# A new order of the same tasks for a fused attention and FFN kernel, from a replay with other transpose times

## The chip, the cores and the metric

The kernel runs on one core of a Trainium2 chip. The time is the device time of one execution in microseconds. TensorE (PE) multiplies matrices, VectorE (DVE), ScalarE (ACT) and GpSimd (POOL) do the rest, and SyncE (SP) issues the transfers.

## The reference

One pre-norm transformer layer on 2048 tokens of width 640, in bf16: multi-query attention with 32 query heads of 20 elements that share one key and one value head, then a gated FFN of width 1536.

```python
q = (x @ wq).reshape(B, S, H, Dh)...          # H = 32, Dh = 20
k = x @ wk;  v = x @ wv                       # one head for all
p = softmax(einsum("bhqd,bkd->bhqk", q, k) * Dh ** -0.5)
attn = einsum("bhqk,bkd->bhqd", p, v)... @ wo
ffn  = (gelu(x @ w_gate) * (x @ w_up)) @ w_down

h  = x + attn(layernorm(x))
h2 = h + ffn(layernorm(h))
```

## The kernel before

The 2048 tokens are cut into 16 tiles of 128 (t = 0 to 15). A *pass* (t, h) is one tile of queries with half of the heads. Its scores are computed transposed, in units of 128 keys by 4 heads of 128 queries (512 columns, one PSUM bank). A *cycle* n is a group of up to five units: `qk_n_0` and `qk_n_1` are its score matmuls on TensorE (line 1257), and `exp_n_0` and `exp_n_1` the exponentials on ScalarE (line 1365) that read two or three banks at once. There are 313 cycles. A part of the keys of each pass (five blocks of 128 in most) takes another way. Its scores (`qkd_n`) become 16-bit patterns of the exponential on VectorE (`db_n`, line 1313), of which two more copies with shifted exponents are made (`ds1_n`, `ds2_n`), either on VectorE (line 1324) or on GpSimd (line 1330). Matmuls with three weighted copies of v (`v_w0` to `v_w2`, GpSimd, line 1933) then sum the three terms.

`pv` are the products with v (line 1481), which gather in one PSUM bank for each pass. At its end `t1`, `rl` (VectorE) and `on` (GpSimd) normalise it, and a DMA transpose turns both halves of a tile (`oT_t`). The output projection `wo` follows on TensorE, then the second layer norm, its transpose `bT_t`, the gate and up matmuls `g` and `u`, the gelu (`sq`, `zk`, `z`, `th`, `h1`, `ph`), a transpose of the product `hT_t`, the down projection `dn` and the store `out_t`.

At the start each tile of x is loaded, normalised (statistics `as1`, `as2` and `aag`, reciprocal `arc`, result `anm_t`), turned by a DMA transpose (`aT_t`) or, for tiles 0, 1 and 5, by TensorE (`atp`, evicted by `ate`), and projected to k and v (`kv_t`, evicted by `ke_t` and `vee_t`). Queries are projected per tile and turned by `qT_t`. All transposes and loads of this kind go through SP's queue, one behind the other. Where TensorE would stand idle there are matmuls on constants, called `warm` and `filler`.

The order of the work on each engine is fixed when the program is built. A planner (`schedule`) first makes an order. `reorder` then replaces it by an order written out in strings: `MOVES` for each engine, `LEFT` for the ds that change between VectorE and GpSimd and for fillers that are dropped, `HEADS` for the head that each `qkd` takes. `retime` replays that order with durations and gives every task a start time; from these come the choice between the two auxiliary PSUM banks (5 and 7), the semaphore waits, and the places at which the streams of SP, ScalarE and GpSimd are split into two blocks. In this replay a transfer that starts before 70 us takes the planner's own duration. A later one took

```python
REAL_DMA = {"qT": 4.6, "bT": 4.0, "oT": 4.1, "hT": 5.0, "out": 4.5}
...
dur = t.dur if at < 70 else self.REAL_DMA.get(t.name.split("_")[0], t.dur)
t.end = landed[e] = max(at + dur, landed[e] + t.serve)
```

where `t.serve` is the least time between two landings of one queue, 0.65 us for the layer norm's transposes. The engines run their streams in order, and each instruction waits on semaphores for what it reads.

Of the kernel before, what the change touches and what calls it, by code (L numbers as in the profile page):

```python
# [15 lines left out]
        "000000000000010000002100101001000161014423010022010432310230553103617279001081106553161006404005"  # L16
        "0444033100"
    ),
    "act": (
        "000000000000001001000200000000000000000000000000000000000000000000000000000000000000000000000000"  # L20
        "00000000000000000000000Y000000000000000000000000000000000J00000000000000000000000000000000000000"
        "000000000000000000g000000000000000000000000000000000000000000000000000d0000000000000000000000000"
        "0000000000000000000000n000000000000000000000000000000000000000000D000000000000000000000000000000"
        "00000Z1300000000000000000000000000000Z1400000000000000000000000000000000000000000000000000000000"
        "00000Z1100000000000000000Z10000000000000000000000000000000000000000000000Z1c000000000000000V0000"
        "0000000000000000000000000000000000Z1300000000000000000000J00000000000000000000000000000000000091"
        "10112000"
    ),
    "pe": (
        "000000000000000000000000000000020011000112543000101152007113210101093210120021333321213399921154"  # L30
        "921242262b123333325e21a3k20111c30300p055Z1hgg5876l665aZ136d77kZ138l8et877686i66e56k6065w70583030"
        "03i006312l0232i222222200b1ag5bmf5na00300008a000a7ooooof11dd1dd223k732b200a2ni322524e32n62120008S"
        "WWZ12Z12m212001k080Z1aZ1aZ1a0Z1bZ1b3i00eu2y024840252Z1UZ1UZ1V3dZ1TZ1V001021r7100q9024061b0Z1IZ1I"
        "Z1K31181wZ1EZ1E43110f00199a608800k08edc0gec103000uaaaccpppp0V09TTUU20m8h1f925nnppp2g011d1511vvvA"
        "2zKK6JLL20711UVVVV260b62c0014Z24Z24Z26Z29Z291Z2qZ2s14Z2qZ2qZ2q10730Z2o0Z2nZ2nZ2nZ2n4d07h02600o10"
        "02c5f40d40Z20Z20g31130Z1UZ1V5o0Z1S030838631051d01b007e1c003000b0301he03488823080eeeff040lllln363"
        "c54Z2lZ2lZ2lZ2nZ2nZ2nZ2nZ2oZ2oZ2oZ2qZ2q5c412b25201c0200Z2gZ2iZ2iZ2i0a0Z2fZ2fZ2fZ2hZ2hZ2hZ2mZ2m26"
        "33f102775061182Z29Z29Z29Z29Z292401Z2bZ2bZ2d1Z2cZ2d12060Z2oZ2oZ2oZ2o10Z2m37708Z2hZ2hZ2hZ2h21bZ2eZ"
        "2eZ2e54060011174384c02321101f1c2e01j22222222Z1BZ1BZ1C02331Z1x223200Z1r0Z1qZ1q42Z1oZ1oZ1oZ1tZ1t22"
        "013e434318j16i8066966600000833g30C02AC23AA4091Z103Z0ZZ11Z11Z12148043a1731yy20254v1uv4242QUUYZ102"  # L40
        "310306802Z1WZ1X0Z1WZ1W01Z2234308400Z2hZ2hZ2hZ2hZ2h7465741Z20Z20Z20Z20Z20c272812j0000a9034Z1OZ1PZ"
        "1P52Z1NZ1N101804036620677771a0020Z1qZ1qZ1qZ1qZ1q070bbbbb07260091b041g2Z19Z192Z18k52Z15Z157k1e9w8"
        "888880c9h578c95777956fma7i5f7555i5de7000003912j00600b3360a390g6a0101lu41t1879912505142332330d01c"
        "0g111057424171617121nn1400jjjl05jjkkk1j6g01a33334400cjfs1F00DD4444500wbv602b08jjjjj0kkq14o221n10"
        "LMM25KK332aZ11Z11Z114eZ11Z157554551438402118a010Z1cZ1d0Z1dZ1dZ1e7301r210x1s1E33331hZ1XZ1X037Z1U3"
        "Z1TZ1TZ1VZ1V14Z1TZ1TZ1UZ1UZ1U042960QQQk630MM5329140h45978995d71430241130b55044407fZ1b01Z19Z190Z1"
        "8Z18Z1aZ1a04Z1a6Z19Z19Z19Z1906631003410lmmmm611UU1c25QQQ1110000681Z14Z14Z14Z14Z163211182142Z10Z1"
        "0Z102b4Z0ZZ0Zf31Z1sZ1s44Z1qZ1tZ1t0231320090Z1B40Z1BZ1BZ1B00Z1z66004307Z2tZ2tZ2tZ2v040Z2sa8203422"
        "41250129614222III6c20JJ33i0026431191060n0e400001ffi3104db65000005003240jjjjj31101tttttZ2HZ2HZ2HZ"
        "2HZ2HZ2H28Z2F51Z2DZ2JZ2M6Z2LZ2NZ30Z30Z32Z32Z32574Z2ZZ2ZZ2ZZ2ZZ30Z303Z2Z452810Z1FZ1HZ1HZ1IZ1I3271"  # L50
        "126840704Z4aZ4aZ4a61Z48Z49164202500Z405Z3ZZ3Z73Z3YZ3Y0732756435Z2xZ2xZ2zZ2zZ2z68Z3HZ3HZ3HZ3HZ3H1"
        "92438221355535105821Z3rZ3rl52Z3oZ3oZ3o700a0092ag16dh06cf55b000800b75500000011Z1G1Z1FZ1GZ1G114Z1I"
        "Z1LZ1LZ1N1Z1MZ1MZ1MZ1M20330405770672303iiiiiZ1OZ1OZ1PZ1PZ1PZ1PZ1PZ1PZ1PZ1PZ1PZ1P523631f225601c5Z"
        "2KZ2KZ2KZ2KZ2K73640145Z2JZ2JZ2JZ2JZ2J06522133000222Z2oZ2oZ2pZ2qZ2q630125990714Z2jZ2j2bZ2hZ2hZ2h3"
        "703121070Z2jZ2kbj1a38Z2eZ2gZ2g0240624001aZ3KZ3KZ3KZ3KZ3KZ3QZ3Q1sZ3OZ3OZ3OZ3TZ3T43717366621521h31"
        "5666c60208Z3BZ3CZ3CZ3CZ3CZ3EZ3E03Z3CZ3CZ3EZ3EZ3E0563035052Z1HZ1HZ1K071Z1H0Z1J30e0Z3jZ3jZ3j010Z3g"
        "Z3g2e00200000hhllp053Z2ZZ2ZZ2ZZ2ZZ2Zb465142Z5dZ5eZ5eZ5eZ5gZ5gZ5g341Z5dZ5fZ5fZ5fZ5g441d6022834302"
        "241128Z4XZ4XZ4XZ4XZ4ZZ4Z1210Z4W4Z4VZ4VZ4WZ4W202a5Z4R10203204192522204180d06Z1Y0Z1X06Z20Z20Z20220"
        "131h171m01h6d0h20Z1S1060dZ1NZ1N5Z1MZ1M6d5aK6hw6g6f6ptk65000006Akssd7gpppahlcb0aaeaZ1mZ1maZ1rZ1uZ"
        "1vb555550648m60000434a93b24e0f3932225Z17Z172Z18Z18Z1921Z2m107Z2lZ2lZ2lZ2l78d030Z2qZ2qZ2qZ3xZ2qZ2"  # L60
        "q40Z3te0Z3rZ3w5Z3v44000223101a1330Z3oZ3oZ3oZ3o2Z3q345Z1RZ1RZ1RZ1RZ1R25556432404dddee0651553Z3iZ3"
        "iZ3l131Z3iZ3k3Z3QZ3QZ3QZ3QZ3Q0Z3P0Z3OZ3OZ3OZ3OZ3OZ3O22Z3GZ3MZ3MZ3OZ3OZ13Z13Z13Z13Z133650Z3IZ3I2Z"
        "3HZ3HZ3JZ3J15Z3HZ3HZ3IZ3IZ3LZ3L7421532431BBBBF283338334202554052Z3hZ3hZ3iZ3iZ3i2441Z3zZ3zZ3zZ3zZ"
        "3z45Z3AZ3CiZ3BZ3D1154Z3zZ3zZ3z110411130e23200209Z3nZ3nZ3n9Z3mZ3m010Z3jZ3jZ3jZ3jZ3jZ3j30Z3h45780h"
# [2079 lines left out]
```

## Time and profile before

| | before |
|---|---|
| median of 3 runs | 732.18 us (729.44 to 733.83) |
| the profiled execution's own time | 730.82 us |
| its span, first to last instruction | 727.4 us |
| busy: TensorE, ScalarE, VectorE, GpSimd | 98%, 95%, 93%, 63% of the span |
| mean granted TensorE clock | 0.998 |
| ScalarE's waits for score matmuls, whole span | 11.5 us in 21 waits |
| transposes on SP's queue | 75 |

All rows come from one profiled execution, and times in them count from its first instruction. In a row of the timeline stand start, length, engine, line, operation, what is written from what, the shape and the number of instructions merged, and in square brackets the idle time before with the one that ended it. A short stall of ScalarE in the middle of the kernel costs its own length, unless a later wait would have held ScalarE anyway.

### The profile page before, as it was taken

How to read it: one execution, taken by the hardware profiler on the slowest of the kernel's cores; microseconds unless marked ns; L12 is line 12 of the kernel's file. 1: busy time of each engine (PE TensorE's matmuls, PEld its weight loads, DVE VectorE, ACT ScalarE, POOL GpSimd, SP SyncE). 2: the span in 40 equal slices, each digit the busy share in tenths (PEclk: the TensorE clock that was granted, in tenths of full speed). 3: DMA queues.
4: the chain of work that ended last, by engine and by line, in shares of the span. 5: the costliest groups of instructions: out<-in, count | busy, mean ns of one | idle time of the engine just before them, and what ended most of it. 6: DMA issues, size and time to landing. Idle time of an engine off the chain costs nothing.

```text
span 727.4 us, 24310 instructions
## 1 busy us (share of the span) xinstructions
PE 709.4 (98%) x10816; PEld 271.5 (37%) x10816; DVE 676.3 (93%) x1261; ACT 691.8 (95%) x667; POOL 459.5 (63%) x366
## 2 busy tenths in 40 slices
PE   8889999999999999999999999999999999999998
PEld 3433333333333333333343434433343333333336
DVE  7878989999999999999999999999999999999895
ACT  4999999999999999999999999999999999999982
POOL 4347483876476867968857565787468765872131
PEclk9999999999999999999999999999999999999999
DMA  6858201112110103030101221121240121012202
GB/s 171 138 184 238 25 2 21 23 27 42 34 25 2 28 6 66 3 58 3 30 23 23 44 23 31 23 49 11 33 57 11 21 53 41 20 11 34 51 5 42
DMA packets 79949, 31.50 MB, mean 43 GB/s; under 512 B 70880, under 2 KB 78560, under 8 KB 79840
## 3 DMA queue, kind: packets, MB, share of 16 engines
q1 hardware_dynamic: 78528, 29.86, 20.6%
q8 instruction: 85, 1.39, 0.9%
q10 hardware_dynamic: 1312, 0.05, 0.1%
q14 instruction: 24, 0.20, 0.1%
HBM read 10.21 MB, written 2.62 MB: 18 GB/s over the span
## 4 chain that ended last, share of the span: by engine, by line
PE 67%; ACT 22%; DVE 5%; DMA 4%; POOL 2%; issue 0%; SPq 0%; DVEq 0%; POOLq 0%
PE ps L900 23%; ACT pbuf L1365 21%; PE ps L1257 21%; PE ps L1481 21%; DVE dbuf L1313 2%; DMA xnT<-xn_tmp 2%; POOL dbuf L1330 1%; DMA onT<-oN 1%; DMA xh<-in_A_x_dram 1%; PE ps L1823 1%; ACT g_z L1646 1%; DVE dbuf L1324 1%; PE ps L1078 0%; PE ps L1842 0%; DVE stats L997 0%
## 5 line engine op out<-in xcount | busy, mean ns | idle before, releaser
L1365 ACT ACTIVATE pbuf<-ps 128x1536 bf16<-128x1536 f32 (+1 forms) x626 | 663.8, 1182 | 12.9 <-PE ps L1257 11.5
L1330 POOL TENSOR_TENSOR dbuf<-dbuf,shifts 128x1024 int32<-128x1024 int32 x170 | 319.7, 1894 | 149.0 <-PE ps L1481 66.9
L1313 DVE TENSOR_SCALAR dbuf<-ps 128x512 int16<-128x512 f32 x608 | 391.5, 683 | 20.8 <-PE ps L1257 17.4
L1257 PE MATMUL ps<-qT,kT 32*128 32x512 bf16 x2048 | 273.2, 385 | 7.7 <-ACT pbuf L1365 2.6
L1481 PE MATMUL ps<-dbuf,v_w 128*32 128x512 bf16 x1824 | 165.0, 384 | 1.0 <-POOL v_w L1933 0.9
L1257 PEld LDWEIGHTS ps<-qT,kT 32*128 32x128 bf16 x2048 | 72.2, 91 | 222.2 <-ACT pbuf L1365 98.1
L1481 PE MATMUL ps<-pbuf,v_ext 128*32 128x512 bf16 (+3 forms) x1928 | 131.0, 329 | 0.4 <-ACT pbuf L1365 0.2
L1324 DVE TENSOR_SCALAR dbuf<-dbuf 128x2048 int16<-128x2048 int16 x134 | 89.9, 698 | 0.6
L1481 PEld LDWEIGHTS ps<-dbuf,v_w 128*32 128x32 bf16 x1824 | 44.1, 95 | 62.3 <-issue 41.4
L900 PE MATMUL ps<-wd_sb,hhT 128*32 128x320 bf16 x1440 | 65.8, 301 | 1.5 <-DVE g_z L1866 0.8
L900 PE MATMUL ps<-wu_sb,xnT 128*32 128x512 bf16 x900 | 64.8, 382 | 0.0
L900 PE MATMUL ps<-wg_sb,xnT 128*32 128x512 bf16 x900 | 63.4, 382 | 0.2
L1481 PEld LDWEIGHTS ps<-pbuf,v_ext 128*32 128x32 bf16 x1928 | 41.5, 95 | 56.6 <-issue 37.7
L1634 POOL TENSOR_TENSOR g_z<-g_gs 128x512 bf16<-128x512 bf16 x45 | 46.5, 1039 | 14.2 <-DVE g_gs L1632 14.0
L1606 POOL TENSOR_TENSOR g_us<-g_z,g_us 128x512 bf16<-128x512 bf16 x24 | 27.4, 1155 | 26.9 <-DVE g_z L1649 26.9
L900 PEld LDWEIGHTS ps<-wd_sb,hhT 128*32 128x32 bf16 x1440 | 33.3, 96 | 24.1 <-issue 9.3
L1640 DVE SCALAR_TENSOR_TENSOR g_us<-ps,g_gs 128x512 bf16<-128x512 f32 x45 | 30.8, 684 | 1.6 <-PE ps L900 1.0
L900 PE MATMUL ps<-wq_sb,xnT 128*32 128x320 bf16 (+1 forms) x660 | 31.3, 297 | 0.3 <-DMA wq_sb<-in_A_wq_dram 0.3
L1632 DVE CAST g_gs<-ps 128x512 bf16<-128x512 f32 x45 | 30.6, 682 | 1.0 <-PE ps L900 0.7
L1507 POOL TENSOR_TENSOR oN<-oT,rL 128x320 bf16<-128x320 f32 x30 | 21.8, 727 | 15.0 <-DVE rL L1502 14.9
L900 PEld LDWEIGHTS ps<-wg_sb,xnT 128*32 128x32 bf16 x900 | 19.2, 95 | 24.5 <-issue 6.8
L1003 POOL TENSOR_SCALAR lnve<-mv 128x1 bf16<-128x1 f32 x31 | 6.8, 222 | 33.6 <-DVE mv L1001 33.3
(117 smaller groups left out, 407.5 us busy)
## 6 DMA issues: line engine op xcount, KB each, us to landing
out_dram<-xh SPq DMA_DIRECT2D x15, 160.0 KB, 2.0
wg_sb<-in_B_w_gate_dram SPq DMA_DIRECT2D x1, 1920.0 KB, 7.4
wd_sb<-in_B_w_down_dram SPq DMA_DIRECT2D x1, 1920.0 KB, 15.6
wu_sb<-in_B_w_up_dram SPq DMA_DIRECT2D x1, 1920.0 KB, 20.0
xh<-in_A_x_dram SPq DMA_DIRECT2D x2, 640.0 KB, 7.3
xh<-in_A_x_dram SPq DMA_DIRECT2D x3, 320.0 KB, 3.2
wq_sb<-in_A_wq_dram SPq DMA_DIRECT2D x2, 400.0 KB, 4.9
wo_sb<-in_A_wo_dram SPq DMA_DIRECT2D x1, 800.0 KB, 9.3
```

Source lines behind the costliest of these rows:

```text
L900: ins = e.matmul(out[r, :], lhs[:, r], rhs, start=start, stop=stop, tile_position=(0, 32 * b))
L1257: return e.matmul(bk.rearrange("p (g n) -> p g n", g=4), kT4[r, kt * P:(kt + 1) * P], qT[r, main_q[t].index, 4 * h:4 * h + 4, :], start=Tr ...
L1313: quad["bits"].append(sc.add("dve", lambda e: e.tensor_scalar(part(seg, w=slice(512 * item[0], 512 * item[0] + 512)), bk(), D_BIAS, 0.0, A ...
L1324: dep = [sc.add("dve", lambda e, j=j, s=s: e.tensor_scalar(part(s), part(seg), D_SHIFT[j], None, ALU.add), 0.602, bits + t_shift, prio=0.4 ...
L1330: dep[0].other = (lambda e, j=j, s=s: e.tensor_tensor(pairs(s), pairs(seg), shifts[:, j - 1:j].to_broadcast([P, 1024]), ALU.add), 2.03)
L1365: exps.append(sc.add("act", lambda e, w0=w0, w1=w1, to=to: e.activation(pbuf[:, to:to + w1 - w0], ps[:, w0:w1], ACT.Exp, scale=EXP_SCALE), ...
L1481: ins = e.matmul(ps[32 * b:32 * b + 32, PVB * 512 + a:PVB * 512 + a + n].rearrange("p (a n) -> p a n", n=32), x[2], span.rearrange("p (a n ...
L1507: onorm[(t, h)] = c = sc.add(by, lambda e: e.tensor_tensor(oN[:, otk.index, h * (D // 2):(h + 1) * (D // 2)].rearrange("p (g l d) -> p l g ...
L1606: return [sc.add("pool", lambda e, c=slice(512 * j, 512 * j + 512): e.tensor_tensor(out[:, k.index, c], a[:, k.index, c], b[:, k.index, c] ...
L1632: ge = sc.add("dve", lambda e, col=col, bk=bk: e.tensor_copy(g_gs[:, gsl.index, col], bk()), d_ps(512), [gm], prio=EVAC + pr, rel=[ax], na ...
L1634: sqt = sc.add("pool", lambda e, col=col: e.tensor_tensor(g_z[:, gsl.index, col], g_gs[:, gsl.index, col], g_gs[:, gsl.index, col], ALU.mult),
L1640: uts.append(sc.add("dve", lambda e, col=col, bk=bk: e.scalar_tensor_tensor(g_us[:, gsl.index, col], bk(), 0.5, g_gs[:, gsl.index, col], A ...
```

## The change

The new order strings are another permutation of the same tasks, with these differences in what runs: three fillers more are kept (127 instead of 130 dropped), 119 instead of 114 ds go from VectorE to GpSimd (17 the other way in both), and 294 of 484 `qkd` take their heads in another sequence. The search that found the order isn't in the file. It used the replay below, and charged early stretches with little TensorE work more. The replay gets new transfer times, one for a transfer alone and one for the distance to the landing before it on the same queue:

```diff
 MOVES = {
     "sp": (
-        "000000000000010000002100101001000161014423010022010432310230553103617279001081106553161006404005"
-        "0444033100"
+        "000000000000010000001000221022100100400330010023200031120031044200257016801007006504205006450005"
+        "0544033100"
     ),
...
-    REAL_DMA = {"qT": 4.6, "bT": 4.0, "oT": 4.1, "hT": 5.0, "out": 4.5}
+    REAL_DMA = {"qT": 3.2, "bT": 3.5, "oT": 2.9, "hT": 4.4, "out": 2.2}
+    BEHIND_DMA = {"qT": 2.3, "bT": 2.0, "oT": 1.6, "hT": 2.6, "out": 0.9}
...
-                dur = t.dur if at < 70 else self.REAL_DMA.get(t.name.split("_")[0], t.dur)
-                t.end = landed[e] = max(at + dur, landed[e] + t.serve)
+                kind = t.name.split("_")[0]
+                late = at >= 70 and kind in self.REAL_DMA
+                t.end = landed[e] = max(at + (self.REAL_DMA[kind] if late else t.dur),
+                                        landed[e] + (self.BEHIND_DMA[kind] if late else t.serve))
```

Decoded, the orders begin to differ as follows (old above new in each pair):

```
TensorE  qk_0_0 warm warm warm warm kv_1 warm warm qk_0_1 qk_1_0 kv_2 atp_5 kv_3 qk_1_1
         qk_0_0 warm kv_1 warm warm warm warm warm qk_0_1 qk_1_0 kv_2 atp_5 kv_3 atp_5 qk_1_1
VectorE  as1_5 aag_3 as2_5 arc_2 qe_0_0 aag_5 as1_4 ate_1 qr_0 ... vee_3 arc_6 ke_3 anm_6
(second) as1_4 aag_3 arc_2 qe_0_0 as1_5 as2_5 ate_1 qr_0 ... ke_3 arc_6 as1_9 arc_7 anm_6 vee_3
GpSimd   ds2_12 v_w0 v_w1 ds1_12 v_w2 ds1_14 ds2_14
         v_w0 v_w1 v_w2 ds1_12 ds2_12 ds2_14
ScalarE  exp_0_0 vee_1 ke_1 exp_0_1 vee_2 ke_2 exp_1_0 exp_1_1 ate_5
         exp_0_0 ke_1 vee_1 exp_0_1 ke_2 vee_2 exp_1_0 ate_5 exp_1_1
SP       qT_0 aT_15 aT_14 qT_1 wg wo wd wu qT_2 oT_0 qT_3 bT_0
         aT_15 aT_14 qT_0 qT_1 wu wd wg wo oT_0 bT_0 qT_3 qT_2
```

(qe_0_0 and qr_0 are the eviction and the turned copy of the first queries.) From there to the end tasks change places with near neighbours.

178 lines of the change are left out of this document (89 added, 89 removed).

## The prediction

> **What bounds the kernel now.** I read the summary of the page first, then the busy times by stretch, then the waits of ScalarE, then the chain of waits, and last the instructions in order of time around each place where the chain leaves ScalarE.
>
> ```profile
> span 727.4 us, 24310 instructions
> PE 709.4 (98%) x10816; PEld 271.5 (37%) x10816; DVE 676.3 (93%) x1261; ACT 691.8 (95%) x667; POOL 459.5 (63%) x366
> ...
> L1365 ACT ACTIVATE pbuf<-ps 128x1536 bf16<-128x1536 f32 (+1 forms) x626 | 663.8, 1182 | 12.9 <-PE ps L1257 11.5
> ```
>
> ScalarE (ACT) is busy 691.8 of 727.4 us, nearly all of it in 626 exponentials of 1.18 us. Its instructions are the same in number and shape after the change, so 691.8 us is a floor, and only the 35.6 us in which it stands idle can be won. The stretches show where they lie (columns: length, then PE, PEld, DVE, ACT and POOL busy, granted TensorE clock, DMA share, GB/s).
>
> ```profile
> 0.00:20.00 20.00, 16.38 (x216) 7.81 (x216) 15.19 (x55) 10.29 (x22) 9.41 (x33) 0.91 0.62 167
> ...
> 550.00:600.00 50.00, 49.50 (x783) 18.87 (x787) 48.44 (x87) 47.20 (x45) 37.88 (x29) 1.00 0.16 30
> ...
> 710.00:727.00 17.00, 13.78 (x239) 11.24 (x235) 9.56 (x27) 4.30 (x8) 1.53 (x2) 1.00 0.31 45
> ```
>
> The first 20 us hold 9.7 us of it, the last 17 us 12.7 us. Between 50 and 700 us ScalarE waits for TensorE only this much:
>
> ```profile
> ACT pbuf L1365 <- PE ps L1257: 7.6, 18, 1.0
> ```
>
> So there are three accounts: the start, 7.6 us in 18 small waits in the middle, and the end. An order can gain a few us in all; it can lose more, since TensorE is 98% busy and takes its work strictly in the written order.
>
> **The change part by part.** The sum is made against the profiled execution, 730.82 us, which is 3.42 us more than its span; the median of the runs, 732.18, is 1.36 us above it, and I add that at the end. What moves is read out of the order strings, each decoded against the planner's list of tasks.
>
> First, GpSimd near 45 us. Its old order is ds2_12, v_w0, v_w1, ds1_12, v_w2; the new one is v_w0, v_w1, v_w2, ds1_12, ds2_12.
>
> ```profile
> 43.20 1.89 POOL L1330 TENSOR_TENSOR dbuf<-dbuf,shifts 128x1024 int32<-128x1024 int32 x1 [10.93 <-DVE dbuf L1313]
> 45.06 1.33 POOL L1933 TENSOR_SCALAR v_w<-v_ext 128x160 bf16<-128x160 bf16 x2
> 46.36 1.89 POOL L1330 TENSOR_TENSOR dbuf<-dbuf,shifts 128x1024 int32<-128x1024 int32 x1
> 48.21 0.61 POOL L1933 TENSOR_SCALAR v_w<-v_ext 128x160 bf16<-128x160 bf16 x1
> ...
> 48.88 0.40 PE L1481 MATMUL ps<-dbuf,v_w 128*32 128x512 bf16 x4 [0.94 <-POOL v_w L1933]
> ...
> 49.86 74.89 ACT L1365 ACTIVATE pbuf<-ps 128x1024 bf16<-128x1024 f32 x71 [0.68 <-PE ps L1257]
> ```
>
> TensorE stands 0.94 us for v_w2, and the next exponential starts 0.68 us late. GpSimd was idle for 10.93 us before ds2_12, so three v_w of about 0.65 us fit into that gap once the evicted v that they read is there. The two ds of 1.89 us then end near 47.0 us (43.20 + 2 x 1.89), before the 48.88 at which the matmul on them ran. What is late next is the last matmul on ds2_12 near 47.1, ahead of the exponential's need. Gain 0.68 us; its bounds are 0 (another wait at that place) and 0.94. After this row ScalarE runs for 74.89 us without a gap, so the gain stays in ScalarE's line at least as far as 124.75 us.
>
> Second, the start. TensorE takes kv_1 after one warming group instead of four; five more follow it, where two did. DVE drops one of two statistics ahead of the cast that the first scores wait for. Neither can be booked as a gain, because ScalarE is held again at 24.37 us:
>
> ```profile
> 12.12 1.45 ACT L1365 ACTIVATE pbuf<-ps 128x1536 bf16<-128x1536 f32 x1 [2.25 <-PE ps L1257]
> 15.34 1.02 ACT L1365 ACTIVATE pbuf<-ps 128x1024 bf16<-128x1024 f32 x1 [1.16 <-PE ps L1257]
> 24.37 24.82 ACT L1365 ACTIVATE pbuf<-ps 128x1536 bf16<-128x1536 f32 x22 [0.52 <-PE ps L1257]
> ...
> 17.63 0.18 DVE L1095 CAST v_ext<-ps 128x20 bf16<-128x20 f32 x1 [0.90 <-PE ps L1080]
> 17.98 0.44 DVE L1018 TENSOR_SCALAR xn_tmp<-xh,mv,lnr 128x640 bf16<-128x640 bf16 x1
> 18.45 4.93 DMA xnT<-xn_tmp
> 23.43 0.45 PE L1078 MATMUL ps<-xnT,wk 128*128 128x128 bf16 x5 [0.78 <-DMA xnT<-xn_tmp]
> ```
>
> The chain there is kv_3, its eviction on DVE at 17.63, the normalisation anm_6 at 17.98, the transpose aT_6 that lands 4.93 us later, kv_6, then qk_4_0. In the new order DVE does ke_3, arc_6, as1_9 and arc_7 between kv_3 and anm_6, where it did vee_3, arc_6 and ke_3. That is one statistics instruction more, and I take 0.4 us for it, from the nearest row on DVE, anm_6 with 0.44. Against it stands an earlier kv_3: DVE idles 0.90 us for it, and the reshuffle before it brings between 0.1 and 0.9. The net is between 0.5 us gained and 0.4 lost. I take 0.15 us lost, near the slower end, because the next rows show most of the reshuffle to run at a reduced clock.
>
> ```profile
> 12.00:14.00 2.00, 2.00 (x33) 1.17 (x34) 2.00 (x7) 1.62 (x3) 0.81 (x3) 0.77 0.36 72
> 14.00:16.00 2.00, 2.00 (x17) 0.47 (x10) 2.00 (x10) 0.84 (x3) 0.47 (x3) 0.50 0.49 95
> 16.00:18.00 2.00, 1.74 (x29) 1.30 (x30) 1.10 (x6) 1.83 (x4) 1.05 (x2) 0.88 0.67 135
> ...
> 13.72 1.04 PE L900 MATMUL ps<-halves,zeros 128*32 128x512 bf16 x8
> ```
>
> The granted clock falls to 0.50 near 13 us and returns by 17. Two warming groups take 1.04 us in it. Five groups at half that each are 2.6 us, so if the clock falls at the same moment the new qk_0_1 starts no earlier than the old. The three fillers more than before (16 instead of 13) lie beside exponentials; at this halved pace they would cost 1.6 us of TensorE, which the 24.37 us hold covers, and if that cover went they would delay one exponential. [...]
>
> Third, the transposes. The replay's times are cut (turned attention output 4.1 to 2.9 us alone, and 1.6 behind another), and the order is moved to fit. What the trace shows from issue to landing (median over all; then the minimum, median and maximum of onT alone):
>
> ```profile
> xnT<-xn_tmp SPq DMA_TRANSPOSE x28, 2.9
> qT<-q_tok SPq DMA_TRANSPOSE x16, 3.2
> onT<-oN SPq DMA_TRANSPOSE x16, 2.6
> hhT<-g_us SPq DMA_TRANSPOSE x15, 3.9
> ...
> DMA to landing us min/median/max: 2.3/2.6/4.6
> ```
>
> The new figures lie just above the medians, the old ones near the maxima. On TensorE the first output projection of a tile comes half a cycle (one exponential, 1.18 us) earlier in tiles 1, 5, 6 and 7 and half a cycle later in tiles 4 and 12. The rest of the projections and FFN groups shift by about a quarter of a cycle on average. On SP's queue qT_0 goes behind aT_15 and aT_14, the weights go wu, wd, wg, wo instead of wg, wo, wd, wu, qT_2 goes behind oT_0, bT_0 and qT_3, and several qT and out transfers swap with their neighbours.
>
> ```profile
> 46.98 6.90 SPq L952 DMA_DIRECT2D wu_sb<-in_B_w_up_dram  x1
> 69.32 1.20 SPq L1514 DMA_TRANSPOSE onT<-oN  x1
> ...
> wu_sb<-in_B_w_up_dram SPq DMA_DIRECT2D x1, 1920.0 KB, 20.0
> ```
>
> The last of the four weight loads landed at 67.0 us (46.98 + 20.0), ahead of the first oT at 69.32 that the first weight, wo, has to meet. They move the same bytes, so wo as the last lands near 67 too. If that 2.3 us of cover went, the first projection would wait for wo. qT_0 is wanted only by the second pass and qT_2 only by tile 2, after all of tile 1. I book nothing for these.
>
> One case can be followed. The worst waits of the middle come from here (rows of the chain of waits, then of TensorE and ScalarE):
>
> ```profile
> 566.37 5.59 POOL dbuf L1330 x3
> ...
> 572.67 4.57 DMA onT<-oN
> ...
> 577.38 0.86 PE L900 MATMUL ps<-wo_sb,onT 128*32 128x320 bf16 x20 [0.34 <-DMA onT<-oN]
> ...
> 576.30 3.36 ACT L1365 ACTIVATE pbuf<-ps 128x1536 bf16<-128x1536 f32 x3 [1.01 <-PE ps L1257]
> 580.30 2.37 ACT L1365 ACTIVATE pbuf<-ps 128x1024 bf16<-128x1024 f32 x2 [0.64 <-PE ps L1257]
> ```
>
> Three ds on GpSimd stand ahead of on_12_1, then its transpose takes 4.57 us. The new order puts a fourth ds (1.86 us each, 5.59 / 3) ahead of on_12_1 and moves the projection back by 1.18. So the projection would wait 0.34 + 1.86 - 1.18 = 1.0 us if the transpose is as slow again, and not at all at the median of 2.6. Bounds for ScalarE are 1.0 lost and 1.65 gained (its two waits, 1.01 + 0.64); I take 0 for this place, between them. For the middle as a whole I take 0 too: the new 2.9 us still leave 0.3 to the median of 2.6, and the two ends are the outer rivals below.
>
> Fourth, five more ds go from DVE to GpSimd (net; some change places). GpSimd gains 5 x 1.86 = 9.3 us on 459.5 busy, DVE loses work. Neither bounds a stretch quoted above, so 0.
>
> Fifth, the end. The new order evicts u14_8 between the two hc_15 on DVE and moves wb1_15 ahead of the first gate matmuls.
>
> ```profile
> 716.44 1.81 PE L900 MATMUL ps<-wd_sb,hhT 128*32 128x320 bf16 x48 [0.78 <-DVE g_z L1866]
> 721.73 3.42 PE L1842 MATMUL ps<-wd_sb,hhT 128*128 128x320 bf16 x24
> ```
>
> TensorE's work in the tail is the same, and both places where it waits or closes (the down projection of tile 14 behind a bank that g_z frees, and the last 24 matmuls) keep their predecessors. I book 0, between 0.5 lost and 0.5 gained.
>
> Sum: 730.82 - 0.68 + 0.15 = 730.29 on the profiled execution; with 1.36 to the median, 731.65, told as 731.6 us. About 0.5% (3.66 us) is what a measurement of this kernel can tell from no change.
>
> **The rivals.**
>
> Faster: the truer transposes let the middle waits go. Two thirds of the 7.6 us vanish, 5.0 us, and the v_w gain stays: 731.6 - 5.0 = 726.6. For it: the waits are small, 18 in number, and the longest follow one late projection. Against it: TensorE itself is 98% busy, and in the stretch from 550 us, where the waits are densest, 49.50 of 50 us.
>
> Slower: the transposes are now given so little time that TensorE, which can't pass a waiting projection, stands before it. The place is the first output projection of tiles 1, 5, 6 and 7. Each is 1.18 us earlier, and a projection that already met its data at the landing hands all of that to ScalarE: 4 x 1.18 = 4.7 us, or 731.6 + 4.7 = 736.3. It decides once those onT take over 2.9 us to land instead of the median 2.6; the 4.57 above shows that some do.
>
> The clock: another early stretch falls under the reduced clock, or the same one lasts longer. In the three stretches above TensorE lost 2 x (0.23 + 0.50 + 0.12) = 1.7 us; a second such dip that nothing covers gives 733.3. [...]
>
> No effect: the edited times touch only the replay, and the orders, being permutations of the same tasks, leave all 18 waits as they are, v_w included: 732.2.
>
> **How the numbers follow.** My forecast gets 0.38, with 729.6 to 733.6 as its own range (the bounds of the start, the projection and the end, 2 us each way). No effect gets 0.08 and the clock 0.15; all three lie within 0.5%, together 0.61. Faster gets 0.20 and slower 0.19. The range reaches into both outer cases, to 727.2 and 736.0, about half of each.
>
> **What would show it.** Right: no wait for v_w near 48 us; the exponential at 24.37 us held by the landing of aT_6 as before, within 0.5 us; the middle waits between 5 and 10 us; the last exponential about 0.5 us earlier. Wrong: waits of TensorE on onT, xnT or hhT of over 1 us in several tiles (slower), or a middle account under 3 us (faster). A dip of the clock beyond 18 us would speak for the clock.

## The result: no change that can be told

| | before | after |
|---|---|---|
| median of 20 runs each | 730.38 us (729.01 to 734.25) | 731.88 us (728.82 to 735.40) |
| ratio after to before, 95% interval | | 1.0005 (0.999 to 1.002) |
| the profiled execution, its span | 730.82, 727.4 us | 734.61, 731.1 us |
| mean granted clock of it | 0.998 | 0.993 |

The forecast was 731.6, and "within 0.5%" the likeliest outcome. Both hold. Working through the steps shows how much of that is luck. Over twenty runs the median of before is 730.38, not the 732.18 of three runs on which the sum was built. Against that median the kernel after is 1.5 us slower, where the steps had promised 0.53 us less. This loss isn't clear of noise either: the ratio on record, 1.0005, isn't the quotient of the two medians (1.0021), and its interval holds 1. The profiled execution of the kernel after, read below, is the second slowest of its twenty, while that of before lies near its median.

The summary of the page after, its row of the exponentials, and ScalarE's waits for score matmuls between 50 and 705 us:

```profile
span 731.1 us, 24330 instructions
PE 710.3 (97%) x10828; PEld 270.3 (37%) x10828; DVE 672.8 (92%) x1256; ACT 692.5 (95%) x667; POOL 468.6 (64%) x371
...
L1368 ACT ACTIVATE pbuf<-ps 128x1536 bf16<-128x1536 f32 (+1 forms) x626 | 664.6, 1178 | 15.9 <-PE ps L1260 14.1
...
ACT pbuf L1368 <- PE ps L1260: 8.8, 21, 1.4
```

(Line numbers after are three higher.) ScalarE's floor stayed, 692.5 us, and its waits for scores grew from 11.5 to 14.1 us. The timeline of ScalarE after has the places; compare with 12.12, 15.34, 24.37 and 49.86 us in the prediction's rows:

```profile
11.96 1.45 ACT L1368 ACTIVATE pbuf<-ps 128x1536 bf16<-128x1536 f32 x1 [1.76 <-PE ps L1260]
14.30 1.02 ACT L1368 ACTIVATE pbuf<-ps 128x1024 bf16<-128x1024 f32 x1 [0.64 <-PE ps L1260]
...
40.09 1.45 ACT L1368 ACTIVATE pbuf<-ps 128x1536 bf16<-128x1536 f32 x1 [1.07 <-PE ps L1260]
...
42.26 3.62 ACT L1368 ACTIVATE pbuf<-ps 128x1024 bf16<-128x1024 f32 x3 [0.72 <-PE ps L1260]
...
47.02 28.72 ACT L1368 ACTIVATE pbuf<-ps 128x1536 bf16<-128x1536 f32 x27 [1.14 <-PE ps L1260]
...
77.17 1.02 ACT L1368 ACTIVATE pbuf<-ps 128x1024 bf16<-128x1024 f32 x1 [1.44 <-PE ps L1260]
...
79.02 37.69 ACT L1368 ACTIVATE pbuf<-ps 128x1024 bf16<-128x1024 f32 x36 [0.82 <-PE ps L1260]
117.59 10.65 ACT L1368 ACTIVATE pbuf<-ps 128x1536 bf16<-128x1536 f32 x10 [0.88 <-PE ps L1260]
```

The hold at 24.37 us and the wait for v_w at 49.86 us are gone. New are three waits between 40 and 48 us, two near 78 and one at 117. Compared exponential by exponential, the kernel after is 1.7 us ahead at cycle 4, 2.1 behind at cycle 13, 4.1 behind at cycle 27, 5.0 at cycle 45, and 3.8 at the last one. So the account of this execution is: start 1.7 won, 40 to 48 us 3.8 lost, near 78 us 2.0 lost, at 117 us 0.9 lost, everything later 1.2 won. That makes the 3.8 us between the two profiled times.

What ends last at these places is in TensorE's timeline (first two rows) and the windows of the trace (length, then PE, PEld, DVE, ACT, POOL busy, clock, DMA share, GB/s):

```profile
39.46 0.59 PE L1260 MATMUL ps<-qT,kT 32*128 32x512 bf16 x5 [1.85 <-DMA qT<-q_tok]
...
75.15 1.45 PE L903 MATMUL ps<-wo_sb,onT 128*32 128x320 bf16 x20 [1.01 <-DVE dbuf L1316]
...
38.00:40.00 2.00, 0.54 (x9) 0.16 (x12) 0.13 (x1) 1.02 (x2) 1.63 (x3) 1.00 0.00 0
...
42.00:44.00 2.00, 2.00 (x16) 0.43 (x13) 1.56 (x4) 1.63 (x2) 0.00 (x0) 0.50 0.29 59
44.00:46.00 2.00, 2.00 (x27) 0.71 (x23) 1.32 (x3) 1.86 (x2) 1.89 (x2) 0.50 0.41 77
...
76.00:78.00 2.00, 2.00 (x30) 0.72 (x23) 0.49 (x1) 0.83 (x1) 0.00 (x0) 0.50 0.00 0
```

TensorE stands 1.85 us for qT_0, whose transpose took 4.00 us; the wait at 75.15, put down to DVE, ends when oT_0 lands at 75.06, 4.49 us after its issue. Each stall is followed by half clock, from 41.14 to 47.97 us and from 75.28 to 78.69, and most of ScalarE's waits lie in those stretches: in this execution 3.8 us were lost where TensorE stood for 1.85.

How many half-clock stretches of about 3.4 us (75.28 to 78.69 us above) a run has can be read from its mean clock, since one of them lowers the mean by 0.5 x 3.4 / 731 = 0.0023. Sorting the runs by it explains most of the spread of these two kernels:

| half-clock stretches | before, 35 runs beside the first experiments | after, 20 runs |
|---|---|---|
| none | 13 runs, mean 729.54 us | 2 runs, 729.18 |
| one | 16, 730.59 | 9, 731.29 |
| two | 6, 731.88 | 5, 733.07 |
| three | none | 4, 733.99 |

One more stretch costs 0.9 to 2.1 us here. Without any, the two orders are equal within 0.4 us, by two runs of the kernel after. That kernel has 1.55 stretches a run and the 35 runs of before 0.80, but before had 0.94, 1.41 and 0.76 when it was timed again beside experiments 5 to 8, 9 to 11 and 12. The 20 runs of before that were timed beside the kernel after have no clock on record; their mean is 730.89 us, against 730.42 for the 35 and 732.06 for the kernel after. So it isn't shown that the new order brings more stretches. For this reason means are given with the experiments, beside medians, and each is to be held against the runs of before that were timed beside it. An order that differs by under 1 us disappears behind whether a stretch occurs.

### The profile page after: what moved, and what is told of

Same layout as the page of the kernel before. It is cut to its first block, busy times and chain, and to the rows that moved or that the text cites. A ratio compares the mean times of both kernels' runs of the same rounds, so it can differ in the third digit from the quotient of the medians.

```text
span 731.1 us, 24330 instructions
## 1 busy us (share of the span) xinstructions
PE 710.3 (97%) x10828; PEld 270.3 (37%) x10828; DVE 672.8 (92%) x1256; ACT 692.5 (95%) x667; POOL 468.6 (64%) x371
## 3 DMA queue, kind: packets, MB, share of 16 engines
q8 instruction: 85, 1.39, 0.8%
## 4 chain that ended last, share of the span: by engine, by line
PE 56%; ACT 30%; DVE 7%; DMA 4%; POOL 1%; issue 1%; SPq 0%; DVEq 0%
ACT pbuf L1368 30%; PE ps L903 19%; PE ps L1260 18%; PE ps L1484 17%; DVE dbuf L1316 3%; DMA xnT<-xn_tmp 2%; DMA onT<-oN 1%; PE ps L1826 1%; ACT g_z L1649 1%; DMA hhT<-g_us 1%; DVE oT L1503 1%; DMA qT<-q_tok 1%; POOL dbuf L1333 1%; DVE xn_tmp L1021 0%; PE ps L1845 0%
## 5 line engine op out<-in xcount | busy, mean ns | idle before, releaser
L1368 ACT ACTIVATE pbuf<-ps 128x1536 bf16<-128x1536 f32 (+1 forms) x626 | 664.6, 1178 | 15.9 <-PE ps L1260 14.1
L1333 POOL TENSOR_TENSOR dbuf<-dbuf,shifts 128x1024 int32<-128x1024 int32 x175 | 329.3, 1896 | 134.4 <-PE ps L1484 80.7
L1484 PE MATMUL ps<-dbuf,v_w 128*32 128x512 bf16 x1824 | 163.2, 384 | 0.0
L1484 PE MATMUL ps<-pbuf,v_ext 128*32 128x512 bf16 (+3 forms) x1928 | 134.4, 331 | 0.5 <-DVE oT L1503 0.5
L1327 DVE TENSOR_SCALAR dbuf<-dbuf 128x2048 int16<-128x2048 int16 x129 | 86.6, 695 | 0.7
L903 PE MATMUL ps<-wo_sb,onT 128*32 128x320 bf16 x600 | 28.5, 312 | 2.3 <-DMA onT<-oN 1.0
```

Of the source, the lines that this page charges most:

```text
L903: ins = e.matmul(out[r, :], lhs[:, r], rhs, start=start, stop=stop, tile_position=(0, 32 * b))
L1327: dep = [sc.add("dve", lambda e, j=j, s=s: e.tensor_scalar(part(s), part(seg), D_SHIFT[j], None, ALU.add), 0.602, bits + t_shift, prio=0.4 ...
L1333: dep[0].other = (lambda e, j=j, s=s: e.tensor_tensor(pairs(s), pairs(seg), shifts[:, j - 1:j].to_broadcast([P, 1024]), ALU.add), 2.03)
L1368: exps.append(sc.add("act", lambda e, w0=w0, w1=w1, to=to: e.activation(pbuf[:, to:to + w1 - w0], ps[:, w0:w1], ACT.Exp, scale=EXP_SCALE), ...
L1484: ins = e.matmul(ps[32 * b:32 * b + 32, PVB * 512 + a:PVB * 512 + a + n].rearrange("p (a n) -> p a n", n=32), x[2], span.rearrange("p (a n ...
```

## The experiments

Each was timed in five rounds (12 runs each). The edits are in the order strings; diffs show them decoded, one engine's order per line.

**1. The new replay times alone, with the old order.**

```diff
-    REAL_DMA = {"qT": 4.6, "bT": 4.0, "oT": 4.1, "hT": 5.0, "out": 4.5}
+    REAL_DMA = {"qT": 3.2, "bT": 3.5, "oT": 2.9, "hT": 4.4, "out": 2.2}
+    BEHIND_DMA = {"qT": 2.3, "bT": 2.0, "oT": 1.6, "hT": 2.6, "out": 0.9}
```

> The order of before with the new transfer times in the replay, nothing moved. If the order alone matters: as before, ratio 1.000 within 0.002, and the same waits of ScalarE (0.5 us for aT_6 near 24 us, 0.7 us for v_w near 50 us). If the choice of auxiliary banks or of the places where the streams are split matters too: over 0.3% away from before.

Measured: 730.81 us, ratio 1.0010 (0.9996 to 1.0025), mean 731.04 with 1.17 stretches a run (before beside experiments 1 to 4: 730.42 and 0.80). The table itself, with the bank choices and split points that follow from it, moves nothing that can be told; what the change does, it does through the order.

**2. The new order with qT_0 alone put back ahead of aT_15; 3. the old order with qT_0 alone put behind aT_14.**

```diff
 SP of the new order
-  aT_15 aT_14 qT_0 qT_1
+  qT_0 aT_15 aT_14 qT_1
 SP of the old order
-  qT_0 aT_15 aT_14 qT_1
+  aT_15 aT_14 qT_0 qT_1
```

> The new order with qT_0 alone put back ahead of aT_15 and aT_14 on SP. If TensorE's stop for qT_0 and the reduced clock behind it eat the gain of the start: no idle time of 1.9 us of TensorE before the score matmuls near 39 us, no reduced clock between 40 and 48 us, 1 to 3 us less than the new order, so 729 to 730.5 us. If transposes given too little time in the middle are the cause: 731.9 us as the new order, and the waits of the middle stay what sets it. If the clock falls at random moments whatever the order: 731.9 us, with the reduced clock somewhere else.

> The order of before with qT_0 alone put behind aT_15 and aT_14. If the place of qT_0 costs what the new order lost there: a wait of ScalarE of about 1 us near 40 us that before has not, 1 to 3 us slower than before (731.5 to 733.5 us). If it is covered, as the prediction booked it: as before, within 0.5 us.

Measured: with qT_0 early in the new order 730.12 us, ratio 1.0000 (0.9987 to 1.0013), mean 730.32 with 0.92 stretches. With qT_0 late in the old order 731.10, ratio 1.0005 (0.9994 to 1.0015), mean 731.17 with 1.58 stretches. ScalarE's timelines, first the new order with qT_0 early, then the old with qT_0 late:

```profile
34.47 38.47 ACT L1368 ACTIVATE pbuf<-ps 128x1024 bf16<-128x1024 f32 x36 [0.31 <-PE ps L1260]
73.14 38.81 ACT L1368 ACTIVATE pbuf<-ps 128x1024 bf16<-128x1024 f32 x37 [0.21 <-PE ps L1260]
113.23 10.65 ACT L1368 ACTIVATE pbuf<-ps 128x1536 bf16<-128x1536 f32 x10 [1.28 <-PE ps L1260]
```

```profile
50.35 1.94 ACT L1365 ACTIVATE pbuf<-ps 128x1024 bf16<-128x1024 f32 x2 [1.33 <-PE ps L1257]
53.14 3.62 ACT L1365 ACTIVATE pbuf<-ps 128x1536 bf16<-128x1536 f32 x3 [0.86 <-PE ps L1257]
57.62 1.02 ACT L1365 ACTIVATE pbuf<-ps 128x1024 bf16<-128x1024 f32 x1 [0.85 <-PE ps L1257]
59.35 69.01 ACT L1365 ACTIVATE pbuf<-ps 128x1536 bf16<-128x1536 f32 x65 [0.71 <-PE ps L1257]
```

With qT_0 early the waits at 40 to 48 us are gone, and those near 78 too, though nothing was moved there. With qT_0 late in the old order ScalarE loses nothing at 40 us; its waits come at 50 to 59 us, in half-clock stretches. TensorE's rows of the same run show what stands ahead of them:

```profile
39.18 0.70 PE L1257 MATMUL ps<-qT,kT 32*128 32x512 bf16 x5 [0.29 <-DMA qT<-q_tok]
...
48.71 0.62 PE L1481 MATMUL ps<-dbuf,v_w 128*32 128x512 bf16 x4 [0.95 <-POOL v_w L1933]
```

The late qT_0 took 2.48 us here, and TensorE waited only 0.29 us for it. The clock falls at 48.66 us, behind the wait for v_w that before has too; experiment 4, with qT_0 in its old place, has a half-clock stretch from 48.51. So this execution doesn't show that the place of qT_0 costs anything in the old order. In the time, the kernel after has a mean 1.17 us above that of before beside it, and with qT_0 early 0.10 us below that of before beside experiment 2: 1.3 us for the place of this transpose in the new order, and 0.75 in the old. Each difference of means from before has a standard error of 0.4 to 0.5 us, worked out from the spread of the runs, so neither is clear of noise.

**4. The new order up to 31 us, then the old; 6. the old order up to 135 us, then the new.**

```diff
 all engines
-  new order throughout
+  4: new order to 31 us (without the late qT_0) | old order from there
+  6: old order to 135 us | new order from there
```

> The new order up to 31 us (the start, with its warming groups, without the later place of qT_0), the old order after it. If the start wins about 1.5 us and the rest of the new order loses it: 728.9 us, 1.5 us below before, and no reduced clock between 13 and 16.5 us. If the start is absorbed by the landing of aT_6, as the prediction booked it: as before within 0.5 us. If the clock alone decides: as before on the median, with runs that differ by 1.7 us for each dip.

> The old order up to 135 us, the new one after it. If the new order wins a little in the middle and loses it before 135 us: about 1.2 us below before (729.2 us), with dips of the clock as rare as in before. If the new order loses through transposes that are given too little time all along: at or above 732 us.

Both have the new replay times as well, which move nothing that can be told (experiment 1). Measured: the new start 730.69 us, ratio 1.0002 (0.9992 to 1.0012). The new rest 732.42, ratio 1.0023 (1.0012 to 1.0035), the one kernel here whose interval lies wholly above 1. In the profile of experiment 4 the hold at 24 us is gone, but waits stand at 49.62 (1.11 us) and 52.26 us (0.70), beside a half-clock stretch. TensorE's wait for v_w, 0.96 us, stands just ahead of them, since the old rest still has it; ScalarE lost 1.81 us there, where it lost 0.68 in before. So what the start won was lost at a place that the new order mends, and the time shows nothing of it. In experiment 6 the waits stand just behind the seam:

```profile
139.58 19.05 ACT L1368 ACTIVATE pbuf<-ps 128x1024 bf16<-128x1024 f32 x18 [1.41 <-PE ps L1260]
159.53 1.03 ACT L1368 ACTIVATE pbuf<-ps 128x1024 bf16<-128x1024 f32 x1 [0.89 <-PE ps L1260]
```

These 2.3 us are more than the 1.6 by which runs without a half-clock stretch exceed those of before (731.02 from three runs against 729.46). So this run can't show a gain of the new order in the rest; with the seam's own wait taken off, it leaves room for 0.7 us.

**5. The old order with the three v_w ahead of ds2_12.**

```diff
 GpSimd of the old order
-  ds2_12 v_w0 v_w1 ds1_12 v_w2
+  v_w0 v_w1 v_w2 ds2_12 ds1_12
```

> The order of before with v_w0, v_w1 and v_w2 alone put ahead of ds2_12 on GpSimd. If that wait was the last one there, as the prediction booked it: no wait of ScalarE near 49 us, 0.7 us less than before (729.7 us). If another wait takes its place (the ds come 0.6 to 1.3 us later for it) or the reduced clock covers it: a wait of 0.3 to 0.7 us at the same exponentials, and the time of before within 0.3 us.

Measured: 729.87 us, ratio 0.9991 (0.9977 to 1.0006), mean 729.95 against 730.44 for before beside it. ScalarE's timeline now runs through the place of the old wait:

```profile
24.82 99.62 ACT L1365 ACTIVATE pbuf<-ps 128x1536 bf16<-128x1536 f32 x93 [0.63 <-PE ps L1257]
```

The wait is gone and nothing is late next up to 124 us. The 0.5 us of time agrees with the 0.68 of the trace, but the interval holds zero as well.

**7. The old order with four of the six warming groups moved into TensorE's idle time ahead of the first scores; 8. the same in the new order, with qT_0 early.**

```diff
 TensorE (old order; in the new one likewise)
-  atp_1 qt_0dve qk_0_0 warm warm warm warm kv_1 warm warm qk_0_1
+  atp_1 warm warm warm qt_0dve warm qk_0_0 kv_1 warm warm qk_0_1
```

> The order of before with four of its six warming groups put into TensorE's idle time between 9 and 12 us, ahead of the first scores (three before the last turned query, one before qk_0_0). If low work in one window of the clock causes the dip at the start: runs at clock 1.0 go from about a third to over two thirds, and the mean falls by 0.6 to 0.9 us. If the moment of the dip is set by something else: clocks and times as before.

> The new order with qT_0 ahead of aT_15 and with the four warming groups moved as in the other kernel. If qT_0 and the start's dip are the two causes: most runs at clock 1.0 and 729.2 us or less, about 1 us below before. If the dips move to other stretches instead: as many as in the new order with qT_0 alone moved (0.9 for each run), 730.2 us.

Measured: 729.48 us, ratio 0.9988 (0.9978 to 0.9999), mean 729.64 with 1.17 stretches in the old order (before beside experiments 5 to 8: 730.44 and 0.94); 729.36, ratio 0.9996 (0.9982 to 1.0011), mean 730.43 with 1.83 stretches in the new. The interval of the first just leaves out 1. Its 0.8 us didn't come in the way that was expected: 3 of its 12 runs have no stretch, against 12 of 35 before, and its runs with one or two (means 729.09 and 729.90) are hardly slower than those with none (729.70). In its profile the clock is halved from 15.36 to 22.19 us. In the new order two runs have five and six half-clock stretches; the profiled one, of 733.81 us, has them from 16 to 33 us:

```profile
18.00:20.00 2.00, 2.00 (x21) 0.85 (x13) 1.08 (x5) 1.08 (x2) 1.23 (x4) 0.50 1.37 209
...
28.00:30.00 2.00, 2.00 (x20) 1.03 (x23) 1.82 (x9) 2.00 (x3) 0.80 (x2) 0.50 0.53 117
```

Moving the groups earlier moved the stretches and didn't abolish them (1.17 and 1.83 a run), and what a stretch cost depended on where it fell: 2.1 us for the first one in the kernel after, by the table above, and none that can be told in experiment 7.

**9. The new order with six fillers ahead of the matmul that waits for qT_0; 10. the old order with the edits of 5 and 7; 11. the new order with qT_0 and qT_2 earlier and the projection of tile 1 later.**

```diff
 9, TensorE of the new order
-  kv_14 qk_10_1 qkd_11 qk_11_0
+  kv_14 qk_10_1 filler filler filler filler filler filler qkd_11 qk_11_0
 11, SP and TensorE of the new order
-  aT_15 aT_14 qT_0 ... oT_0 bT_0 qT_3 qT_2
+  qT_0 aT_15 aT_14 ... qT_2 oT_0 bT_0 qT_3
+  wo_1: first half behind qk_45_1, second behind qk_46_0
```

> The new order unchanged but for six fillers (about 0.26 us each at full clock, 1.6 us) that TensorE does ahead of the qkd of cycle 11, where it stands 1.85 us for the late qT_0. The transpose, and so the wait, stay. Theory A (the late qT_0 costs by the clock: too little work in a window, then 6.8 us at half clock): no half-clock stretch starts near 41 us, and no waits of ScalarE at 42 and 47 us; about 1.2 to 1.7 us of mean less than the changed kernel's 732.1, near 730.6, as when qT_0 itself was put first. Rival B (the stall itself costs, the clock does not): nothing changes, 732.0 within 0.4, and the waits at 42 to 48 us stay. Rival C (the six fillers overrun the landing of qT_0 or run at half clock themselves): the wait near 40 us grows by up to 1.6 us, 732.5 to 733.

> The order before with both edits that by themselves came out under it: the three v_w ahead of ds2_12, and four of six warming groups moved into TensorE's idle time ahead of the first scores. If the two gains (0.5 and 0.8 us of mean) are of different places and add up: 729.1 within 0.4 (ratio 0.998). If they are one and the same thing, or run-to-run luck with the clock's windows: 729.5 to 730.4, no better than either alone.

> The new order with three places put right: qT_0 ahead of aT_15, qT_2 ahead of oT_0, and the output projection of tile 1 two and a half score groups later, since its transpose took 4.05 to 4.45 us in each profile of this order. Theory (the losses of the new order lie at these places, the rest is equal): 729.4 to 730.0, no wait of ScalarE over 0.5 us between 35 and 125 us. Rival (the transposes and the clock only find other places): 730.1 or more, as with qT_0 alone.

Measured: experiment 9 729.81 us, ratio 0.9983 (0.9964 to 1.0002), mean 729.74; 10 729.27, ratio 0.9971 (0.9954 to 0.9988), mean 729.35; 11 731.39, ratio 1.0001 (0.9981 to 1.0020), mean 731.31. Each has 0.83 stretches a run; before beside them has a mean of 731.26 with 1.41.

Experiment 10 is the best version, 0.29% under before by its ratio; the change as it is was not timed beside it. Its expectation of adding up held. Much of the gap lies in the stretches, though: the runs without any differ by 0.4 us (729.15 against 729.52), and five of the 29 runs of before have four. Experiment 11 missed. With the projection of tile 1 later, its second half, a wait of 0.59 us and gate matmuls stand between two groups of scores (113.06 and 115.60 us on TensorE), and ScalarE waits for the second of them:

```profile
116.03 1.02 ACT L1368 ACTIVATE pbuf<-ps 128x1024 bf16<-128x1024 f32 x1 [1.51 <-PE ps L1260]
```

Experiment 9 came out lower than its own theory (730.6), and its profile shows why the theory was not what it tested. TensorE's row of the fillers, and what the turned queries took from issue to landing between 30 and 50 us (two of them), in experiment 9, where the smaller is qT_0, and then in the kernel after, where it is the larger:

```profile
37.75 1.48 PE L903 MATMUL ps<-halves,zeros 128*32 128x512 bf16 x24
...
DMA to landing us min/median/max: 2.5/3.0/3.4
```

```profile
DMA to landing us min/median/max: 3.0/3.5/4.0
```

qT_0 took 2.5 us instead of 4.0 and landed at 37.60, before the fillers began. There was nothing left to cover. Transposes of the attention output were fast as well: those of tiles 0 and 1 took 2.56 us where they had taken 4.49 and 4.05. What the edit had changed for these two is the count of TensorE's instructions ahead of these places, and the DMA tables of the trace led on. The transfers during the turned output of tile 0 in the kernel after, issue to landing cut into 40 slices, and their queues:

```profile
GB/s 0 0 0 0 0 0 0 0 0 146 46 194 198 208 212 178 87 18 0 0 0 0 0 0 7 7 11 9 9 9 9 18 235 78 0 0 0 0 0 0
...
q8 instruction: 1, 0.02, 2.2%
q14 instruction: 1, 0.01, 0.5%
...
onT<-oN SPq DMA_TRANSPOSE x1, 4.5
```

The bulk of the transpose is done at mid-time, then next to nothing moves (7 to 11 GB/s), then the last part comes in one burst. In that time a packet of 0.02 MB ran on the queue that the table calls "instruction"; by its share it took 2.2% of 16 engines for 4.49 us, or 1.6 us of one. The same view of the same transfer in experiment 12, below, lists no such packet and has one unbroken block:

```profile
GB/s 0 0 0 0 0 0 0 0 0 0 0 0 0 0 0 0 0 0 68 175 227 215 223 223 207 235 179 235 203 188 116 48 8 0 0 0 0 0 0 0
...
q1 hardware_dynamic: 672, 0.16, 32.3%
...
onT<-oN SPq DMA_TRANSPOSE x1, 2.6
```

For qT_0 the count had not changed, since the fillers come behind it. In the kernel after a q8 packet began at 37.31 us, 1.98 us behind the issue; in experiment 9 one began at 37.47, 2.35 us behind the issue and 0.13 ahead of the landing. So 0.4 us in the timing, not the edit's mechanism, freed this transpose.

**12. The new order, with six warming groups more in TensorE's idle time near 10 us and nothing else.**

```diff
+    def warm_groups(e):
+        warms.append(0)
+        for _ in range({15: 2, 16: 4, 18: 3}.get(len(warms), 1)):
+            r = strips(e, bank(PVB), zeros[:], ...)
+        return r
 TensorE of the new order (the 15th and 16th groups moved, six more emitted)
-  qt_0dve qk_0_0 warm kv_1 warm warm warm warm warm qk_0_1
+  warm*2 qt_0dve warm*4 qk_0_0 warm kv_1 warm*3 warm warm qk_0_1
```

> The new order with six warming groups more (24 pairs of weight load and matmul) in the 1.6 us near 10 to 11.5 us in which TensorE stands idle anyway; qT_0 stays behind aT_14 and nothing is put where TensorE waits for it. All that TensorE runs later lies 48 instructions further on in its stream, exactly as behind the six fillers of the run before. Theory F (a transpose is slow when a transfer of instructions, one 16 KB packet on one of the 16 DMA engines, falls into it; the place of that packet is set by the count of TensorE's instructions, not by the order): the landings of onT repeat those with the fillers and not those of the changed kernel: tiles 0 and 1 near 2.56 us (were 4.49 and 4.05), tile 6 near 4.4 (was 2.59), tile 9 near 4.8 (was 3.40); qT_0 lands about 2.5 us after its issue (was 4.0), the wait of 1.85 us for it is under 0.4, no half-clock stretch at 41 or 75 us, no wait of ScalarE near 77 or 117; mean 728.5 to 729.8. Theory A (the fillers helped by covering a wait for qT_0 that the order itself brings): qT_0 takes 4.0 us again, the wait of 1.0 to 1.85 us and the half clock near 41 us come back, onT of tiles 0 and 1 take 4.0 to 4.5: 731.5 to 732.3.

Measured: 730.26 us, ratio 1.0001 (0.9987 to 1.0015), mean 730.12 with 0.75 stretches (before beside it: 730.18 and 0.76). The turned outputs, issue to landing in us:

| tile | 0 | 1 | 2 | 6 | 8 | 9 | 15 |
|---|---|---|---|---|---|---|---|
| after | 4.49 | 4.05 | 2.57 | 2.59 | 4.21 | 3.40 | 3.75 |
| 9, fillers at 37.75 us | 2.56 | 2.56 | 2.59 | 4.40 | 3.68 | 4.80 | 2.31 |
| 12, groups at 10 us | 2.57 | 2.56 | 4.13 | 4.28 | 3.36 | 5.19 | 2.30 |

Experiment 12 has nothing where experiment 9 had its fillers, and nearly the same transposes are slow, tile 2 apart. Theory F is borne out in the landings of the turned outputs. It missed on qT_0, which took 3.31 us and not 2.5, behind a slow aT_14. It holds less well in the time: 730.12 lies between the two forecasts, nearer to its own. ScalarE and TensorE show what is left:

```profile
32.17 5.97 ACT L1368 ACTIVATE pbuf<-ps 128x1536 bf16<-128x1536 f32 x5 [0.53 <-PE ps L1260]
39.05 83.12 ACT L1368 ACTIVATE pbuf<-ps 128x1024 bf16<-128x1024 f32 x79 [0.92 <-PE ps L1260]
...
38.12 0.45 PE L1081 MATMUL ps<-xnT,wk 128*128 128x128 bf16 x5 [1.30 <-DMA xnT<-xn_tmp]
```

A packet now falls into aT_14, which took 4.28 us, and TensorE waits 1.30 us for that, with no half-clock stretch behind it. ScalarE then runs 83 us without a gap, through 78 and 117 us.

## Why the prediction came out right, step by step

- **v_w order (0.68 won): right.** The wait near 48 us is gone in the kernel after and in experiment 5, where it was worth 0.5 us of mean, with an interval that holds zero. Where a half-clock stretch follows this wait, as in the profiles of experiments 3 and 4, it costs more: ScalarE's waits there sum to 3.75 and 1.81 us. GpSimd did the three v_w in one piece in its idle gap:

```profile
37.80 1.90 POOL L1936 TENSOR_SCALAR v_w<-v_ext 128x160 bf16<-128x160 bf16 x3 [6.00 <-DVE v_ext L1098]
```

- **The start (0.15 lost): wrong in sign.** The assumption that failed is that the clock falls at the same moment, 13 us. In the profiled execution after it stayed at 1.00 from 12 to 20 us, and the exponential held by aT_6 started at 22.65 instead of 24.37 us, with no wait. That is 1.7 us won, outside the bounds of 0.5 won to 0.4 lost, and 1.6 of it came after the first exponential. Most of this is luck with the clock: in experiments 2, 4 and 9, which have the same start, the clock did fall, at 11.41, 10.96 and 12.61 us, and the same stretch of work won only 0.3, 0.7 and 0.5 us. The hold by aT_6 is gone in these runs too (at most 0.04 us). In the time the start alone gives nothing that can be told (experiment 4, 1.0002).
- **qT_0 behind aT_14 (0): the term that was mis-sized most.** "Wanted only by the second pass" was true, but the first matmul of that pass stands in TensorE's order ahead of the rest of cycle 11, where TensorE arrives at 39.46 - 1.85 = 37.6 us, and nothing passed it. In the profiled execution that is a stall of 1.85 us, with 3.8 us lost around it; in the time it is 1.3 us of mean (experiment 2), not clear of noise. The prediction had asked what the transfer was moved past, and not when its first reader comes up. The replay's new times would not have warned either, as they apply from 70 us on. Part of the cause is not the order at all: the transpose took 4.0 us with an instruction packet 1.98 us behind its issue. Where it took 2.48 us, in experiment 3, TensorE waited 0.29 us.
- **Weights (0): right.** The wait at 75.15 us is for oT_0, not for wo.
- **First projections earlier in tiles 1, 5, 6 and 7, the slower rival:** real at tile 1 alone (waits of 0.88, and 1.28 in experiment 2). The transposes of tiles 5, 6 and 7 landed in 2.57, 2.59 and 2.56 us and cost nothing. The rival's condition, over 2.9 us, was the right one. It was met at tile 1, with 4.05 us and an instruction packet in it.
- **on_12_1 (0, between 1.65 won and 1.0 lost): inside the bounds, but the reading behind them was wrong.** Four ds now run ahead of it as foreseen, the transpose took 3.11 us, and TensorE didn't wait for it. In place of 1.01 and 0.64 ScalarE waits 0.40 us there. But the exponential that waited 1.01 us started at 576.30, ahead of the projection at 577.38, so the projection can't have held it. Experiment 1, with the old order, shows it from the other side: its transpose of tile 12 took 2.59 us in place of 4.57, and the waits stay:

```profile
575.51 3.28 ACT L1368 ACTIVATE pbuf<-ps 128x1536 bf16<-128x1536 f32 x3 [1.01 <-PE ps L1260]
579.22 2.37 ACT L1368 ACTIVATE pbuf<-ps 128x1024 bf16<-128x1024 f32 x2 [0.43 <-PE ps L1260]
```

  The slow transpose cost 0.2 us (0.64 against 0.43). Nor does the gain behind cycle 45 come from here: from cycle 250 to 260 the kernel after wins 0.2 us on before, and by cycle 200 it had already won 1.4.
- **Five ds to GpSimd (0): right.** 468.6 us busy there, 9.1 more (9.3 worked out), and no wait from it.
- **The end (0): right.** From the row of negm to the end of the span it is 727.4 - 708.27 = 19.13 us before and 731.1 - 712.05 = 19.05 after:

```profile
708.27 0.28 ACT L1762 ACTIVATE negm<-ps 128x128 f32<-128x128 f32 x1 [1.83 <-PE ps L1750]
```

```profile
712.05 0.28 ACT L1765 ACTIVATE negm<-ps 128x128 f32<-128x128 f32 x1 [1.95 <-PE ps L1753]
```

- **The middle (7.6 us, expected between 5 and 10): 8.8.** The faster rival, two thirds of it gone, didn't come about; of the 8.8, 3.1 are the three waits near 78 and at 117 us.
- **The clock rival: right in kind.** Half-clock stretches beyond 18 us occurred, at two places of the profiled execution (41.14 and 75.28 us). It was priced at 1.7 us a dip; by the table above the first three cost 2.1, 1.8 and 0.9 us in the kernel after, while in experiment 7 they cost next to nothing. Whether the new order brings more of them than the old isn't shown.
- **The last addend (1.36 us to the median): wrong.** It was taken from three runs; over twenty the median of before is 0.44 us below its profiled execution. This error of 1.8 us upwards and the missing 2.0 us (0.53 forecast as won, 1.5 lost by the medians) hide each other; that the forecast came within 0.3 us is luck.

What stays open: how much of the loss at qT_0 is its place and how much the packet. In experiment 9 the late qT_0 met the packet only at its end, and the fillers stood beside it; in experiment 12 a packet fell on aT_14, right ahead of it. Open too is whether the new order is slower at all over many runs, what experiment 6 would give without its seam, and what makes the clock fall in one run and not in the next.

## What to carry to other kernels

When a transfer is moved back in its queue, look for its first reader in the consumer's written order, not for the pass that it belongs to. A stall of TensorE under 2 us is worth pricing with the half-clock stretch that may follow it (here 1.85 us, with 6.83 us at half clock behind it). And when an edit changes the number of instructions ahead of a place, compare the landing of every transpose behind it before believing that the edit's own mechanism made the difference (with 48 instructions more in experiment 12, oT_0 took 2.57 us in place of 4.49). Hold each experiment against the runs of before that were timed beside it: here the mean of before moved by 1.1 us from one such set to another.

## What the runs showed of the hardware

**Transposes were slow where an instruction packet began in them.** The 14 traces (before, after and twelve experiments) hold 224 transposes of the attention output. In 126 of them no packet of the queues called "instruction" began between issue and landing: none took over 2.84 us. In the other 98 one did: 75 took over 3 us, up to 5.19. A longer transfer has more time to meet a packet, so the count was made again for the first 2.56 us behind the issue alone: in 95 a packet began there, among them all 75 slow ones, and in 129 none. The 63 whose packet began between 0.4 and 2.2 us behind the issue all took over 3.1 us; later or earlier ones are mixed. The page of the kernel after lists these queues:

```profile
q8 instruction: 85, 1.39, 0.8%
...
q14 instruction: 25, 0.20, 0.1%
```

1.39 MB in 85 packets are 16.4 KB each; TensorE's 10828 matmuls and 10828 weight loads, divided by 85, are 255 instructions for each packet. That the packets of q8 are TensorE's is the author's estimate, from this quotient and from experiment 12, where 48 instructions more for TensorE changed which transposes were slow; no trace shows whose they are. The counts above show slow transposes and packets together, and not how one holds up the other.

**The clock fell without a full pause of TensorE.** Busy time of TensorE in the 3.41 us ahead of a half-clock stretch, as long as the stretch from 75.28 to 78.69 us, from the kernel before (first row) and after:

```profile
9.66:13.07 3.41, 1.67 (x23) 0.64 (x24) 3.41 (x15) 1.16 (x3) 1.85 (x5) 1.00 0.10 34
```

```profile
37.73:41.14 3.41, 1.66 (x33) 0.80 (x37) 1.27 (x2) 2.34 (x3) 1.84 (x3) 1.00 0.00 0
...
71.87:75.28 3.41, 2.33 (x34) 0.74 (x30) 3.13 (x6) 3.41 (x4) 2.37 (x2) 1.00 0.85 46
```

1.66 to 2.33 us of work in 3.41 did not keep the clock up. Work alone doesn't decide it, though. In experiment 2 the clock fell at 11.41 us; the 3.41 us that start 29 such lengths later have less work than the last row and were followed by no stretch (the execution's mean clock, 0.998, leaves room for the one at 11.41 alone):

```profile
110.40:113.81 3.41, 1.98 (x48) 1.08 (x47) 2.04 (x4) 2.13 (x3) 0.78 (x1) 1.00 0.06 10
```

The starts of the two stretches after, 41.14 and 75.28 us, are 34.14 us apart, ten times 3.41. That is one spacing in one execution, and it doesn't show what sets the moment of a stretch. The windows of the clock in the expectations of experiments 7, 9 and 10 are the author's assumption, which no run here shows. In the rows above the longest single wait of TensorE ahead of a stretch was 1.85 us; what is enough to bring one no run here shows.
